# A score quad's fifth product moves to another PSUM bank, and the builder's list puts the quads' products ahead by a microsecond

## The chip, the cores and the metric

The kernel runs on one core of one Trainium2 chip. The metric is device time in microseconds (us), the median of three runs. TensorE is called PE, ScalarE ACT, VectorE DVE, GpSimd POOL; SP issues most DMAs.

## The reference, cut to what matters

One conformer block over x of shape (2, 4000, 512), all in bfloat16: a feed-forward layer, attention without heads over 4000 tokens, a convolution of three taps, and a second feed-forward layer, with layer norms between.

```python
h = _layernorm(x); h = _silu(h @ w_ff1_a) @ w_ff1_b
x1 = x + 0.5 * h
h = _layernorm(x1)
q = h @ w_q; k = h @ w_k; v = h @ w_v
scores = jnp.einsum('btd,bsd->bts', q, k) * scale
p = _softmax(scores, axis=-1)
attn = jnp.einsum('bts,bsd->btd', p, v) @ w_o
x2 = x1 + attn
...                       # convolution with gate, normalised over all tokens: x3
h = _layernorm(x3); h = _silu(h @ w_ff2_a) @ w_ff2_b
return _layernorm(x3 + 0.5 * h)
```

## The kernel before

**Tiling.** The 8000 tokens are cut into 16 chunks of 512, eight for each batch; the eighth of each batch has 416 (function `width`). Scores are computed with keys on the partitions and one chunk's queries on the free axis, 32 tiles of keys (`kt`) to a chunk (`g`).

**Stages.** The first feed-forward stage runs to about 430 us of the profile, the attention to about 1398, a short stage that finishes the convolution to about 1440, and the second feed-forward stage to the end. Convolution and layer norms of earlier chunks are laid beside the attention of later ones.

**A seven-product scheme.** Most large products use a Strassen-like scheme with seven half-size products in place of eight. In chunks that do not open a batch ("not plain", 14 of 16), four key tiles at a time form a *score quad* (`score_quad`, L1993): 7 quads to a chunk, 98 in all, each done in 4 steps, one for each `kt`. Each of its seven products is a block of 4 matmuls, 128 x 256 (128 x 208 in the two short chunks), two halves of the bank by two halves of the contraction.

**Banks of a quad.** It uses three of PSUM's eight banks: c is bank 0, x is bank 1, h is bank 2. The profile calls all of them s; y is used for the products with V and other work. Step 0: product 5 opens h, ACT copies it to m5 in SBUF, product 1 opens c, ACT copies c over h. Step 1: product 6 adds to h, DVE writes h + m5 into x (`plus`), product 2 adds to c, ACT takes the exponential of c. Step 2: product 7 adds to h, DVE writes h + m5 over m5, product 3 adds to x, ACT takes the exponentials of x and of m5. Step 3: product 4 adds to h, ACT takes its exponential. In the profile m5 has the tile name xt; the products read so: 5 and 6 are s<-xt, 1 and 2 are s<-work,keys, 7 and 4 are s<-xt,keys, 3 is s<-work,xt. DVE's sum into x is s<-s,xt, that into m5 is xt<-s,xt.

**Opening a bank.** A matmul with `start=True` opens a bank: it overwrites. Where an engine has written the bank since, a matmul with `start=False` adds to that only in columns that a matmul has written since the bank was last opened. Product 3 adds so to x, bank 1. Two users of bank 1, `q_group` (L1637) and `pw1` (L2405), write only 416 columns of it when their chunk is short; `touch` (L968) then adds a matmul of 96 columns over the rest.

**Other users of banks 0 to 2.** In chunks with quads, `sbank` gives out banks 0 and 1 in steps where quads do not hold them, and `self.bank(1)` is used by the tail keys' scores and one convolution product.

**Products with V** (`pv`, L1837) are seven forms for each pair of key tiles, into banks 3 to 7. They read the exponentials, or sums of them that DVE makes (`pair_sums`, L1796), and V or its sums, of which two forms are streamed from DRAM (xt<-v12d).

**Order of the work.** The program writes its operations into a list; a builder, `Plan`, then orders them for each engine before anything runs. A block of matmuls that ends with an increment of PE's semaphore is a node. In `once` (L272), the builder goes through the list with estimated durations; `choose("PE")` (L289) takes, among nodes whose inputs are done and that lie no more than `beside` (8000 ns) behind the head of the list, the one that can start first. Among those that can start at the same moment it takes the earliest of the list, by its number k. T[k] is the sum of the estimated PE durations ahead of node k. Other engines are ordered by how late a node may be. The best of six passes is emitted. At run time every engine goes through its own queue in order and waits on semaphores.

Every instruction is issued from one helper, so all rows of the profile have line L93; they are told apart by tiles.

Of the kernel before, what the change touches and what calls it, by code (L numbers as in the profile page):

```python
# [9 lines left out]
AF = mybir.ActivationFunctionType  # L10
AX = mybir.AxisListType

B, T, D, F, KW = 2, 4000, 512, 2048, 3
# [4 lines left out]
CHUNK = TPC * TILE  # L18
# [3 lines left out]
NCK = B * TCB  # L22
# [39 lines left out]
class Ev:  # L62
    __slots__ = ("key", "val", "snap")
# [21 lines left out]
class Call:  # L85

    __slots__ = ("name", "args", "kw")
# [16 lines left out]

class Node:

    __slots__ = ("e", "emit", "dur", "land", "preds", "succs", "left", "ready", "late", "at", "seq", "ev", "size", "turn", "other")


class Plan:  # L110
# [7 lines left out]
    def __init__(self, sync, ahead, beside):  # L118
        self.S, self.ahead, self.beside = sync, ahead, beside
        self.nodes, self.pe, self.block = [], [], []  # L120
        self.w, self.r, self.d = {}, {}, {}
        self.table, self.same, self.first = None, [], None

    @staticmethod
    def size(ap):
# [47 lines left out]
    def new(self, e, dur, land, emit, reads, writes, dkeys=()):  # L173
        n = Node()
        n.e, n.dur, n.land, n.emit, n.preds, n.succs, n.seq, n.at = e, dur, land, emit, set(), [], len(self.nodes), len(self.pe)
        n.size, n.turn, n.other = 0, False, None
        self.nodes.append(n)
        n.preds |= self.link(n, reads, writes, dkeys)
        return n
# [92 lines left out]
    def once(self):  # L272

        pe, T = self.pe, self.T
        for n in reversed(self.nodes):
            if n.e != "PE":
                n.late = min([s.late - self.lag(n, s) - (self.SPARE if n.size else 0) for s in n.succs] + [pe[min(n.at, len(pe) - 1)].late + 40000])
        free = {e: 0.0 for e in self.AFTER}
        wait = {e: [] for e in self.AFTER}
        for n in self.nodes:  # L280
            n.left, n.ready = len(n.preds), 0.0
            if not n.left:
                for e in n.other or (n.e,):
                    wait[e].append(n)
        head, done, starts = 0, [False] * len(pe), [0.0] * len(pe)
        index = {n: k for k, n in enumerate(pe)}
        order, pipe = [], 0.0

        def choose(e):  # L289
            if e == "PE":  # L290
                best = None
                for n in wait["PE"]:
                    k = index[n]
                    if T[k] - T[head] > self.beside:
                        continue
                    key = (max(free[e], n.ready - (40 if k == head else 0)), k)
                    if best is None or key < best[0]:
                        best = (key, n)
                return best and (max(free[e], best[1].ready), best[1])
            limit = T[head] + self.ahead  # L300
            found = [n for n in wait[e] if T[n.at] <= limit]
            if not found:
                return None
            now = max(free[e], min(n.ready for n in found))
            can = sorted([n for n in found if n.ready <= now], key=lambda n: (n.late, n.seq))
            soon = [n for n in found if n.ready > now]
            for n in can:
                end = now + max(n.other[e][0] if n.other else n.dur, n.size / 260) + self.OVER[e]
                if all(end <= u.ready + 60 or u.late >= end or u.late >= n.late for u in soon):
                    return now, n  # L310
            u = min(soon, key=lambda n: n.ready)
            return max(free[e], u.ready), u

        ask = dict.fromkeys(free, True)
        said = {}
        while len(order) < len(self.nodes):
            for e in free:
                if ask[e]:
                    said[e], ask[e] = choose(e), False
            e, (s, n) = min([c for c in said.items() if c[1]], key=lambda c: c[1][0])  # L320
            for o in n.other or (e,):
                wait[o].remove(n)
                ask[o] = True
            if n.other:
                self.take(n, e)
            free[n.e] = s + n.dur + self.OVER[n.e]
            order.append((n, e))
            if n.size:
                begin = max(s + (400 if n.turn else n.dur + 400), pipe)
                pipe = begin + n.size / (180 if n.turn else 260)  # L330
                n.land = pipe - s + 1000
            if n.e == "PE":
                k = index[n]
                done[k], starts[k] = True, s
                if k == head:
                    while head < len(pe) and done[head]:
                        head += 1
                    ask = dict.fromkeys(free, True)
            for u in n.succs:
                lag = self.lag(n, u)  # L340
                u.ready = max(u.ready, s if lag is None else s + lag)
                u.left -= 1
                if not u.left:
                    for o in u.other or (u.e,):
                        wait[o].append(u)
                        ask[o] = True
        return free["PE"], order, starts


class Sync:  # L350
# [125 lines left out]
    def emit_dma(self, engs, dkey, fns, reads, writes):  # L476

        req = self._required(reads, writes)
        prev = self.count[dkey]
        if prev > 0:  # L480
            v = req.get(dkey)
            if v is None or v.val < prev:
                req[dkey] = Ev(dkey, prev, {})
        for e in dict.fromkeys(engs):
            self._emit_waits(e, req)
        for e, fn in zip(engs, fns):
            fn(self.eng[e]).then_inc(self.sem[dkey], 16)
            self.count[dkey] += 16
        snap = dict(self.clock[engs[0]]) if len(set(engs)) == 1 else {}
        ev = Ev(dkey, self.count[dkey], snap)  # L490
        self._bind(ev, reads, writes)
        return ev

    def planned(self, ahead, beside):
        self.plan = Plan(self, ahead, beside)
# [55 lines left out]
class Conformer:  # L551
# [412 lines left out]
    def mm(self, out, lhsT, rhs, start, stop, reads, bank, inc=None, **kw):  # L964
        self.S.op("PE", lambda e: e.matmul(out, lhsT, rhs, start=start, stop=stop, **kw),
                  reads=reads, writes=[bank], inc=stop if inc is None else inc)

    def touch(self, ps, b_ps, W):  # L968
        if W < CHUNK and b_ps is self.bank(1)[1]:
            x = self.hT[0][:, 0, 0, :]  # L970
            self.mm(ps[:, W:CHUNK], x, x[:, 0:CHUNK - W], False, True, [self.b_hT[0][0]], b_ps, skip_group_check=True)

    def warm(self, n):

# [662 lines left out]
    def q_group(self, b, qc, dc):  # L1637

        s, sl = qc % 2, self.query_slot(b, qc)
        ps, b_ps = self.sbank()  # L1640
        W = width(qc)
        lin, lo = self.queries(qc, sl)
        for cc in range(DC):
            self.mm(ps[:, 0:W], self.M[:, cc, dc * 128:(dc + 1) * 128], lin[:, cc, lo:lo + W],
                    cc == 0, cc == DC - 1, [self.b_M] + self.b_lnT[sl], b_ps)
        self.touch(ps, b_ps, W)
        self.act(self.qT[s][:, dc, 0:W], ps[:, 0:W], AF.Copy, [b_ps], [self.b_qT[s][dc]])

    def queries(self, qc, sl):
# [343 lines left out]
    def score_quad(self, g, q, step):  # L1993
# [32 lines left out]
                 reads=[b_h, b_m5], writes=[b_out])  # L2026

        if step == 0:
            product(5, h, b_h, True)
            self.act(m5, h[:, 0:W], AF.Copy, [b_h], [b_m5])  # L2030
            product(1, c, b_c, True)
            self.act(h[:, 0:W], c[:, 0:W], AF.Copy, [b_c], [b_h])
        elif step == 1:
            product(6, h, b_h)
            plus(x[:, 0:W], b_x)
            product(2, c, b_c)
            exp(c[:, 0:W], b_c, 11)
        elif step == 2:
            product(7, h, b_h)
            plus(m5, b_m5)  # L2040
            product(3, x, b_x)
            exp(x[:, 0:W], b_x, 12)
            exp(m5, b_m5, 22)
        else:
            product(4, h, b_h)
            exp(h[:, 0:W], b_h, 21)
# [2 lines left out]

    def attention(self, old, hook):  # L2050

        for g in range(NCK):
            W, plain = width(g), g % TCB == 0
            for kt in range(KT):
# [4 lines left out]
                if plain and kt < KT - 1 or kt < 2 or kt == KT - 2:  # L2059
# [3 lines left out]
                    else:  # L2063
                        self.act(self.P30[:, 0:W], ps[:, 0:W], AF.Exp, [b_ps], [self.b_P30], scale=SCALE)
                elif not plain and kt < KT - 2:
                    self.score_quad(g, *divmod(kt - 2, 4))
                if g == 0 and kt < 2:
                    self.pop(old // 2 if kt == 0 else old - old // 2)
                if kt == (24 if g else 21):
# [335 lines left out]
    def pw1(self, t, cb, bank=None):  # L2405
# [9 lines left out]
        for out, x in moves:  # L2415
            for cc in range(DC):
                self.mm(out, self.Wp1[:, cc, cb * 128:(cb + 1) * 128], x[:, cc], cc == 0 and out is moves[0][0], cc == DC - 1,
                        [self.b_Wp1] + self.b_lnT[1 if t == NCK - 1 else 0], b_ps, skip_group_check=True)
        if t < NCK - 1:
            self.touch(ps, b_ps, W)  # L2420
        return ps, b_ps

    def taps_beside(self, t, cc):
# [603 lines left out]
```

## Time and profile before

| What | Value |
|---|---|
| Runs | 1884.49 us median of 3 (1883.29 to 1886.34) |
| Profiled execution | 1882.47 us, its span 1878.7 us |
| Granted TensorE clock | 1.0 |
| Matrix products issued | 15389 |

A row of the time order gives start, length, engine, operation, "out<-in" by tile names, shape and count, and in brackets the idle time of the engine before it and what ended that. Consecutive like instructions are merged. A row of a matmul lasts from its start to the end of its drain, so rows overlap when PE is dense. Rows of groups give count, busy us, mean ns of one, and idle time before them.

### The profile page before, as it was taken

How to read it: one execution, taken by the hardware profiler on the slowest of the kernel's cores; microseconds unless marked ns; L12 is line 12 of the kernel's file. 1: busy time of each engine (PE TensorE's matmuls, PEld its weight loads, DVE VectorE, ACT ScalarE, POOL GpSimd, SP SyncE). 2: the span in 40 equal slices, each digit the busy share in tenths (PEclk: the TensorE clock that was granted, in tenths of full speed). 3: DMA queues.
4: the chain of work that ended last, by engine and by line, in shares of the span. 5: the costliest groups of instructions: out<-in, count | busy, mean ns of one | idle time of the engine just before them, and what ended most of it. 6: DMA issues, size and time to landing. Idle time of an engine off the chain costs nothing.

```text
span 1878.7 us, 39230 instructions
## 1 busy us (share of the span) xinstructions
PE 1860.1 (99%) x15389; PEld 1442.7 (77%) x15389; DVE 1463.0 (78%) x3191; ACT 1306.9 (70%) x2419; POOL 133.2 (7%) x301
## 2 busy tenths in 40 slices
PE   9999999999999999999999999999998999999998
PEld 5888888866777777777677777777774888888886
DVE  7888888868667777776777677768778888888885
ACT  5777777644667777677667677777668687777773
POOL 1000000000000000000000000000011000000000
PEclk9999999999999999999999999999999999999999
DMA  7323344197545555447944444444375222222111
GB/s 191 101 79 91 80 113 105 57 265 214 173 144 151 158 170 166 107 133 177 248 125 133 130 122 114 122 137 121 111 203 171 74 61 71 77 46 61 49 43 33
DMA packets 325014, 231.52 MB, mean 123 GB/s; under 512 B 204179, under 2 KB 295638, under 8 KB 324566
## 3 DMA queue, kind: packets, MB, share of 16 engines
q1 hardware_dynamic: 324294, 228.68, 44.4%
q8 instruction: 123, 2.02, 0.4%
q14 instruction: 69, 0.57, 0.1%
q10 hardware_dynamic: 528, 0.26, 0.0%
HBM read 128.44 MB, written 55.79 MB: 98 GB/s over the span
## 4 chain that ended last, share of the span: by engine, by line
PE 97%; DVE 1%; ACT 1%; DMA 0%; issue 0%; DVEq 0%; ACTq 0%
PE s L93 48%; PE y L93 48%; DVE work L93 1%; ACT work L93 0%; DMA xt<-v12d 0%; DVE wff L93 0%; DVE xt L93 0%; DVE s L93 0%; ACT sums L93 0%; DMA work<-work 0%; ACT wff L93 0%; ACT keys L93 0%; ACT s L93 0%; ACT xt L93 0%; ACT L93 0%
## 5 line engine op out<-in xcount | busy, mean ns | idle before, releaser
L93 ACT ACTIVATE sums<-s 128x512 bf16<-128x512 f32 (+2 forms) x494 | 288.2, 584 | 171.3 <-PE s L93 169.9
L93 ACT ACTIVATE keys<-s 128x512 bf16<-128x512 f32 (+2 forms) x284 | 165.6, 588 | 183.6 <-PE s L93 166.4
L93 DVE TENSOR_TENSOR sums<-sums 128x512 bf16<-128x512 bf16 (+3 forms) x528 | 195.4, 398 | 75.0 <-ACT sums L93 70.0
L93 PE MATMUL y<-work,keys 128*128 128x256 bf16 x1920 | 244.6, 273 | 0.0
L93 PE MATMUL s<-work,keys 128*128 128x256 bf16 (+5 forms) x1456 | 224.5, 292 | 0.0
L93 ACT ACTIVATE work<-xt,work 128x512 bf16<-128x512 bf16 x268 | 206.7, 785 | 7.8 <-DVE work L93 7.8
L93 PE MATMUL y<-wff,keys 128*128 128x256 bf16 (+3 forms) x1592 | 209.1, 276 | 0.1
L93 PEld LDWEIGHTS y<-work,keys 128*128 128x128 bf16 x1920 | 187.8, 98 | 25.1
L93 PE MATMUL y<-sums,keys 128*128 128x256 bf16 (+1 forms) x1440 | 202.6, 270 | 0.0
L93 PE MATMUL s<-sums 128*128 128x256 bf16 x1296 | 193.8, 273 | 0.0
L93 DVE TENSOR_TENSOR keys<-keys 128x1024 bf16<-128x1024 bf16 (+2 forms) x262 | 169.2, 662 | 28.8 <-ACT keys L93 13.6
L93 PE MATMUL y<-work,wff 128*128 128x256 bf16 (+2 forms) x1116 | 184.0, 292 | 0.0
L93 PEld LDWEIGHTS y<-wff,keys 128*128 128x128 bf16 (+1 forms) x1592 | 151.2, 98 | 32.4 <-issue 3.3
L93 DVE BATCH_NORM_STATS2 work<-xt 128x6 f32<-128x512 bf16 x251 | 163.9, 680 | 5.1 <-DMA xt<-in_x_dram 4.3
L93 PEld LDWEIGHTS s<-work,keys 128*128 128x128 bf16 (+1 forms) x1456 | 119.2, 97 | 50.6 <-ACT sums L93 4.0
L93 PEld LDWEIGHTS y<-sums,keys 128*128 128x128 bf16 x1440 | 138.8, 98 | 24.1 <-DVE sums L93 0.6
L93 POOL TENSOR_TENSOR work<-work 128x4 f32<-128x4 f32 (+3 forms) x107 | 89.8, 840 | 807.4 <-DVE work L93 804.9
L93 PE MATMUL s<-work,wff 128*128 128x512 bf16 (+5 forms) x668 | 141.0, 345 | 3.2 <-DVE work L93 2.7
L93 PEld LDWEIGHTS s<-sums 128*128 128x128 bf16 x1296 | 126.7, 98 | 20.0
L93 PE MATMUL s<-work 128*128 128x512 bf16 (+4 forms) x565 | 138.5, 375 | 3.0 <-DVE work L93 1.8
L93 PE MATMUL y<-sums,xt 128*128 128x256 bf16 (+1 forms) x960 | 139.4, 270 | 1.5 <-DVE sums L93 0.8
L93 PEld LDWEIGHTS y<-work,wff 128*128 128x128 bf16 x1116 | 108.2, 98 | 29.8
(143 smaller groups left out, 3202.2 us busy)
## 6 DMA issues: line engine op xcount, KB each, us to landing
xt<-kfd SPq DMA_DIRECT2D x98, 384.0 KB, 3.3
xt<-v12d SPq DMA_DIRECT2D x105, 256.0 KB, 2.9
xd<-xt SPq DMA_DIRECT2D x28, 512.0 KB, 3.1
xt<-xd SPq DMA_DIRECT2D x28, 512.0 KB, 4.3
out_dram<-xt SPq DMA_DIRECT2D x14, 512.0 KB, 3.0
xt<-in_x_dram SPq DMA_DIRECT2D x13, 512.0 KB, 4.0
dcvd<-wff SPq DMA_DIRECT2D x48, 128.0 KB, 2.1
keys<-dcvd SPq DMA_DIRECT2D x12, 512.0 KB, 4.3
```

Of the source, the lines that this page charges most:

```text
L93: return getattr(eng, self.name)(*self.args, **self.kw)
```

## The change

Three edits go together. In `score_quad`, product 5 opens bank x (bank 1) instead of h, and ACT's copy to m5 reads it there. `touch` and its two calls are left out; product 5 now opens bank 1 over the quad's whole width before product 3 adds to it. And nodes made while a quad's step is written into the list carry `front` = 1000 (ns); among nodes that can start at the same moment, `choose` now takes the smallest T[k] - front.

```diff
@@ class Plan
+        self.front = 0
@@ def new
-        n.size, n.turn, n.other = 0, False, None
+        n.size, n.turn, n.other, n.front = 0, False, None, self.front
@@ def once, choose
-                    key = (max(free[e], n.ready - (40 if k == head else 0)), k)
+                    key = (max(free[e], n.ready - (40 if k == head else 0)), T[k] - n.front)
@@ class Sync
+    def front(self, ns):
+        if self.plan:
+            self.plan.front = ns
@@ class Conformer
-    def touch(self, ps, b_ps, W):
-        if W < CHUNK and b_ps is self.bank(1)[1]:
-            x = self.hT[0][:, 0, 0, :]
-            self.mm(ps[:, W:CHUNK], x, x[:, 0:CHUNK - W], False, True, [self.b_hT[0][0]], b_ps, skip_group_check=True)
@@ def q_group
-        self.touch(ps, b_ps, W)
@@ def score_quad
         if step == 0:
-            product(5, h, b_h, True)
-            self.act(m5, h[:, 0:W], AF.Copy, [b_h], [b_m5])
+            product(5, x, b_x, True)
+            self.act(m5, x[:, 0:W], AF.Copy, [b_x], [b_m5])
             product(1, c, b_c, True)
             self.act(h[:, 0:W], c[:, 0:W], AF.Copy, [b_c], [b_h])
@@ def attention
                 elif not plain and kt < KT - 2:
+                    S.front(1000)
                     self.score_quad(g, *divmod(kt - 2, 4))
+                    S.front(0)
@@ def pw1
-        if t < NCK - 1:
-            self.touch(ps, b_ps, W)
```

More of the change, by code (lines that the diff above doesn't have):

```diff
@@ L105 @@
 class Node:
-    __slots__ = ("e", "emit", "dur", "land", "preds", "succs", "left", "ready", "late", "at", "seq", "ev", "size", "turn", "other")
+    __slots__ = ("e", "emit", "dur", "land", "preds", "succs", "left", "ready", "late", "at", "seq", "ev", "size", "turn", "other", "front")
 class Plan:
@@ L2050, in attention @@
     def attention(self, old, hook):
+        S = self.S
         for g in range(NCK):
```

## The prediction

> **What bounds the kernel now.** I read the head of the page, its chain that ended last, and busy time by stretches (us, busy time and count of PE, PEld, DVE, ACT and POOL, granted clock, DMA share, GB/s).
>
> ```profile
> span 1878.7 us, 39230 instructions
> ...
> PE 1860.1 (99%) x15389; PEld 1442.7 (77%) x15389; DVE 1463.0 (78%) x3191; ACT 1306.9 (70%) x2419; POOL 133.2 (7%) x301
> ...
> PE 97%; DVE 1%; ACT 1%; DMA 0%; issue 0%; DVEq 0%; ACTq 0%
> ```
>
> ```profile
> 200.00:300.00 100.00, 100.00 (x918) 89.63 (x916) 89.61 (x184) 75.97 (x131) 8.06 (x8) 1.00 0.41 102
> 460.00:895.00 435.00, 432.13 (x3588) 326.92 (x3586) 320.81 (x731) 301.64 (x598) 25.27 (x83) 1.00 0.56 154
> ...
> 960.00:1398.00 438.00, 435.22 (x3673) 331.99 (x3673) 320.37 (x707) 309.95 (x609) 27.97 (x101) 1.00 0.45 127
> 1398.00:1440.00 42.00, 36.72 (x203) 17.55 (x202) 34.30 (x77) 28.97 (x53) 8.37 (x23) 1.00 0.66 210
> 1500.00:1600.00 100.00, 100.00 (x868) 84.65 (x866) 86.12 (x180) 77.48 (x136) 8.07 (x8) 1.00 0.25 70
> ```
>
> TensorE (PE) sets the end: 97% of the chain, at a granted clock of 1.00. The two feed-forward stages (200 to 300, 1500 to 1600) have no gap. The fourteen query chunks with score quads are the stretches 460 to 895 and 960 to 1398. There PE looks 99% busy, but a matmul's row contains its drain, which hides small stalls. So I went to the order of time:
>
> ```profile
> 757.33 0.61 PE L93 MATMUL s<-xt 128*128 128x256 bf16 x4
> 757.78 0.60 PE L93 MATMUL s<-work,keys 128*128 128x256 bf16 x4
> 758.05 0.70 DVE L93 TENSOR_TENSOR s<-s,xt 128x512 f32<-128x512 f32 x1 [1.20 <-PE s L93]
> 758.22 0.60 PE L93 MATMUL y<-sums,xt 128*128 128x256 bf16 x4
> ...
> 758.81 0.61 PE L93 MATMUL s<-xt,keys 128*128 128x256 bf16 x4
> 759.25 0.60 PE L93 MATMUL s<-work,xt 128*128 128x256 bf16 x4
> ...
> 759.69 1.03 PE L93 MATMUL s<-work,wff 128*128 128x512 bf16 x4
> ...
> 760.55 0.60 PE L93 MATMUL s<-xt,keys 128*128 128x256 bf16 x4
> ```
>
> This is one quad's products 6 (757.33), 2 (757.78), 7 (758.81), 3 (759.25) and 4 (760.55). Undisturbed, four 256-wide matmuls take 0.44 us of PE (757.33 to 757.78), 0.109 each, though a row of four lasts 0.60: a stall shows as idle only for what exceeds some 0.165. Product 7 starts 0.59 after the group before it, 0.15 late. It writes bank h, which VectorE (DVE) must have read. Product 6 is issued by 757.77; DVE starts 0.28 later, takes 0.70, and product 7 follows 0.06 behind: **1.04 us from 6 to 7**, in which PE needs other work, the cover. Here it had two groups, 0.87.
>
> ```profile
> PE s L93 <- DVE s L93: 2.3, 6, 0.4
> PE s L93 <- DVE xt L93: 1.5, 3, 0.6
> PE y L93 <- DVE sums L93: 0.8, 2, 0.4
> PE y L93 <- DMA xt<-v12d: 0.6, 1, 0.6
> ```
>
> ```profile
> 499.76 0.50 PE L93 MATMUL s<-xt,keys 128*128 128x256 bf16 x3 [0.21 <-DVE s L93]
> ...
> 1386.65 0.53 PE L93 MATMUL s<-xt,keys 128*128 128x208 bf16 x4
> ```
>
> The first four rows are all of PE's visible waits from 455 to 1400 (total, times, longest): 5.2 us in 12, with the hidden 0.165 each 7.2. Setting every start against the dense spacing, I find some 11 us of stalls there, apart from those at the 32-row tiles of the tail keys. Product 7 has the most: 17 stalls, 4.5 us, the first 0.37 (499.76), the last 0.22 (1386.65).
>
> **Part 1: product 5 goes to bank x.** Before, it opened bank h and so waited until ScalarE (ACT) had read product 4 of the quad before. Now it opens x, free once product 3's exponential has read it. No instruction is added.
>
> ```profile
> 761.19 0.60 ACT L93 ACTIVATE sums<-s 128x512 bf16<-128x512 f32 x1 [0.19 <-PE s L93]
> 761.42 0.61 PE L93 MATMUL y<-sums,keys 128*128 128x256 bf16 x4
> ...
> 761.93 0.60 PE L93 MATMUL s<-xt 128*128 128x256 bf16 x4
> ```
>
> Product 5 at 761.93 is 0.07 late (0.51 after a group of 0.44): product 4 (from 760.55) was issued by 760.99, and the exponential's 0.60 lies between. There are 13 such delays, 1.1 us together. In the new order product 3 leads the next product 5 by 0.7 us at least and 3.9 in the median. I take **0.9 gained**; bounds 0 and 1.1.
>
> The wait goes to what used bank 1 last. In 36 quads that is a projection or a convolution product, which DVE reads and the queue of PE, in order, now stands behind:
>
> ```profile
> L93 DVE SCALAR_TENSOR_TENSOR xt<-s,work,xt 128x512 bf16<-128x512 f32 x59 | 44.0, 746 | 14.4 <-PE s L93 14.4
> ```
>
> 0.28 + 0.75 + 0.06 is 1.09 of need, against covers of 1.06 to 1.09 in the new order: **0.3 lost**, bounds 0 and 1.1 (0.03 in each).
>
> **Part 2: quads' products lead by a microsecond.** Among groups that could start at the same moment, the builder now takes the one with the earliest place in the list, where a quad's product counts 1000 ns earlier. The new order of PE leaves the first feed-forward stage as it was up to its last chunks; in the second a few groups change place, where nothing stalls. Between them nearly every chunk is reordered, with the same matmuls. So I count the cover in each order, at 0.109 us for each 256-wide matmul. The two short chunks, with 208 columns, have their own rows:
>
> ```profile
> 874.23 0.53 PE L93 MATMUL s<-xt 128*128 128x208 bf16 x4
> 874.59 0.52 PE L93 MATMUL s<-work,keys 128*128 128x208 bf16 x4
> 875.52 0.53 PE L93 MATMUL s<-xt,keys 128*128 128x208 bf16 x4 [0.41 <-DVE s L93]
> ```
>
> Product 6 takes 0.36 (0.089 a matmul), and 7 follows its issue at 874.59 by 0.93: the need there.
>
> Product 6 to 7: the old order is short of 1.03 us (0.93 in the short chunks) in 17 of 98 quads, by 4.45 us, which agrees with the 4.5 seen. The new one is short in three quads, by 0.3, and in four by 0.05 since m5 comes late. **4.0 gained**, bounds 3.0 and 4.2.
>
> Product 1 to 6 goes through ACT's copy of c to h:
>
> ```profile
> 763.23 0.60 PE L93 MATMUL s<-work,keys 128*128 128x256 bf16 x4
> 763.67 0.60 PE L93 MATMUL s<-sums,keys 128*128 128x256 bf16 x4
> 764.10 0.60 PE L93 MATMUL y<-sums,keys 128*128 128x256 bf16 x4
> 764.56 0.61 PE L93 MATMUL s<-xt 128*128 128x256 bf16 x4
> ```
>
> Two groups of cover (763.67, 764.10) leave product 6 late by 0.02, so 0.89 is needed. In the new order 27 quads have just these 0.87 and one 0.44, 1.1 us short together against 0.2 in the old: **0.9 lost**, bounds 0.6 and 1.2. Product 7 to 4 needs what 6 to 7 needs; three quads of the short chunks now lack 0.62 together, against 0.06: **0.6 lost**, bounds 0 and 0.6.
>
> The Trainium skill speaks against counting cover so: "TensorE: Matmul & The Clock Gate", section Back-to-back issue gap, gives some 131 ns per 512-wide matmul in a stream of weight loads and matmuls. By it, product 3 and one such group would cover an estimated 0.96 us between 7 and 4, some 0.07 short in every quad that has just these. The trace differs: from 759.69 to 760.55 four of them take 0.86, 0.215 each.
>
> **Part 3: products with V, and the rest.**
>
> ```profile
> 502.57 0.38 PE L93 MATMUL y<-sums,xt 128*128 128x256 bf16 x2 [0.45 <-DVE sums L93]
> ...
> 1376.81 0.35 PE L93 MATMUL y<-sums,xt 128*128 128x208 bf16 x2 [0.64 <-DMA xt<-v12d]
> ```
>
> Products with V that come early wait for DVE's sums over a quad's exponentials: three stalls, 1.3 us, the first 0.61 (502.57). From product 4 to the first of them the new order has 6.8 us of PE work in the mean instead of 5.5, and 0.7 at least instead of 0.2. **1.2 gained**, bounds 0 and 1.3. The wait for V's transfer (1376.81, 0.81) stays: in that place the release of its buffer leads its use by 4.6 us in both orders.
>
> ```profile
> 781.80 0.42 ACT L93 ACTIVATE work<-work 128x256 bf16<-128x256 bf16 x1 [2.72 <-DMA work<-work]
> ...
> 784.18 0.61 PE L93 MATMUL s<-xt,keys 128*128 128x256 bf16 x4 [0.51 <-DVE xt L93]
> ```
>
> In four chunks product 4 of the first quad is late (2.2 us together), as at 784.18: ACT stood behind a transposing transfer, and DVE behind ACT. Nothing in the change speeds that transfer up: 0, bounds 2.2 either way.
>
> ```profile
> L93 PE MATMUL s<-keys 128*128 128x96 bf16 x5 | 1.0, 204 | 0.0
> ```
>
> The removed matmuls are these five: 96 columns at 0.109 per 256 are 0.04 each, **0.2 gained**, bounds 0 and 1.0.
>
> **The sum.** Gains 0.9 + 4.0 + 1.2 + 0.2 = 6.3, losses 0.3 + 0.9 + 0.6 = 1.8: 4.5 us. The profiled execution took 1882.5 us, its span and 3.8 around it, so 1878.0; the median shown lies 2.0 above it, at 1884.5, so I forecast **1880.0**.
>
> **Rivals.** *More of it goes.* Quads that run earlier may also lift the four late product 4s and the last 0.9 of product 5 and V: of some 11 us about 9.5 would go, giving 1875. For it: the covers grow nearly everywhere. Against it: the transfer is no part of the change.
>
> *The stalls only move.* Covers are PE work; they suffice only if DVE and ACT take each operation at once, and these are 73 and 70% busy in the stretches. If one in ten of the 98 quads finds a 0.4 to 0.7 us operation ahead of its sum, 10 x 0.5 gives 5 back: 1884.5. Against it: in the old order covers alone explain product 7's stalls to 0.1 us.
>
> *Slower: bank 1's reader.* In the 36 quads of part 1 the margin is nil. If DVE has one operation of 0.69 ahead of that read, product 5 and all PE work behind it are that much later. From 7 such quads the gain is gone (7 x 0.69 = 4.8); at 13 the kernel is slower by over 0.2%; at half of them, 18 x 0.69 - 4.5 gives 1892. For it: DVE, unlike ACT in the old place, reads most projections behind other sums. Against it: before, product 1 stood behind the same reader on bank 0, and stalls there come to 0.2 us.
>
> **How the numbers follow.** The forecast gets 0.52, more of it 0.14, no net change 0.24, the slower case 0.10. About 0.2%, 3.8 us, is what a measurement of this kernel can tell from no change. Gains over it: 0.44 of the forecast's 0.52 and the whole second case, 0.58; within it the other 0.08, the third case's 0.22 and a little of the last: 0.30; slower 0.12. The forecast's own bounds are 1875.5 to 1883.5. The range 1874.5 to 1887.5 takes in the second case and the third, and leaves out the slow end.
>
> **What would show it.** Right: the visible waits of PE for DVE s fall from 2.3 us to below 0.5; product 5's matmuls (s from xt) follow their predecessor at 0.44; rows for s from keys with 96 columns are gone; many product 6 rows 0.02 late. Wrong: idle time before s from xt released by DVE xt or DVE work at chunks' steps with projections, sums on DVE that start over 0.3 after product 6, or new stalls in the stage after the last chunk (now 1398 to 1440), which should keep its gaps of 5.3 us. The forecast falls if the stretches 460 to 895 and 960 to 1398 together do not shrink by 2 us or more.

## The result, and the profile after

The changed kernel took 1878.73 us (median of 9 runs, 1877.09 to 1879.83) against 1883.55 us before (9 runs, 1882.21 to 1886.34): a ratio of 0.9975, 95% interval 0.9967 to 0.9984. The profiled execution took 1879.46 us, its span 1875.7.

The head of its page, and busy time by stretches (columns as before):

```profile
span 1875.7 us, 39058 instructions
...
PE 1851.9 (99%) x15271; PEld 1444.6 (77%) x15384; DVE 1465.4 (78%) x3188; ACT 1309.2 (70%) x2421; POOL 134.6 (7%) x302
```

```profile
460.00:895.00 435.00, 431.16 (x3573) 329.24 (x3604) 324.05 (x734) 303.25 (x601) 23.36 (x83) 1.00 0.56 154
960.00:1393.00 433.00, 430.13 (x3617) 330.60 (x3645) 318.27 (x701) 308.99 (x607) 29.48 (x101) 1.00 0.45 129
1393.00:1436.00 43.00, 37.62 (x200) 18.36 (x202) 34.77 (x76) 28.86 (x52) 9.45 (x24) 0.96 0.65 205
```

This trace lacks 113 matmul rows (15271, where 15384 weights were loaded), so PE's busy time reads some us too low and proves nothing here. What can be read is when things happen. The last matmul of the chunks with score quads started at 1397.94 us before and starts at 1393.22 now, so 4.7 us went there. The stage behind it keeps its gaps (43.00 - 37.62 = 5.4 us, 5.3 before), but from that matmul to the end of the span 1.7 us more pass than before: in this execution the granted clock is 0.5 for 3.4 us from 1428.2 us on (hence the 0.96 in the row above), which costs some 0.8 us, and the new order waits 0.66 us for ACT before the matmul at 1445.46. Hence 3.0 us in the spans.

The same quad's place in the order of time:

```profile
751.88 0.60 PE L93 MATMUL s<-xt,keys 128*128 128x256 bf16 x4
752.32 0.60 PE L93 MATMUL s<-xt 128*128 128x256 bf16 x4
...
754.31 0.61 PE L93 MATMUL s<-xt 128*128 128x256 bf16 x4
754.76 0.60 PE L93 MATMUL s<-work,keys 128*128 128x256 bf16 x4
...
755.19 0.60 PE L93 MATMUL s<-sums,keys 128*128 128x256 bf16 x4
...
755.63 0.38 PE L93 MATMUL y<-sums,xt 128*128 128x256 bf16 x2
...
755.85 0.60 PE L93 MATMUL s<-xt,keys 128*128 128x256 bf16 x4
```

Product 5 (752.32) follows product 4 of the quad before at 0.44, without a wait for its exponential. Between product 6 (754.31) and product 7 (755.85) stand two and a half groups instead of two, 1.09 us from the issue of 6 (754.76 to 755.85), and 7 is on time. PE's visible waits from 455 to 1400 us:

```profile
PE s L93 <- DVE xt L93: 2.3, 3, 1.8
PE s L93 <- ACT sums L93: 0.4, 2, 0.3
PE s L93 <- ACT s L93: 0.4, 1, 0.4
```

The waits for DVE s (2.3 us) are gone, and so are those of the products with V. Most of what is left is one stall of product 4, in the first quad of the chunk at 835 us:

```profile
835.66 2.75 SPq L93 DMA_TRANSPOSE work<-work  x2
...
841.85 0.42 ACT L93 ACTIVATE work<-work 128x256 bf16<-128x256 bf16 x1 [3.46 <-DMA work<-work]
...
844.30 0.53 PE L93 MATMUL s<-xt,keys 128*128 128x208 bf16 x4 [1.84 <-DVE xt L93]
```

### The profile page after: what moved, and what is told of

The parts are those of the page before. It is cut to its first block, busy times and chain, and to the rows that moved or that the text cites. A ratio compares the mean times of both kernels' runs of the same rounds, so it can differ in the third digit from the quotient of the medians.

```text
span 1875.7 us, 39058 instructions
## 1 busy us (share of the span) xinstructions
PE 1851.9 (99%) x15271; PEld 1444.6 (77%) x15384; DVE 1465.4 (78%) x3188; ACT 1309.2 (70%) x2421; POOL 134.6 (7%) x302
## 3 DMA queue, kind: packets, MB, share of 16 engines
q8 instruction: 123, 2.02, 0.4%
## 4 chain that ended last, share of the span: by engine, by line
PE 95%; ACT 2%; DVE 1%; DMA 1%; issue 1%; POOL 0%; SPq 0%; DVEq 0%; ACTq 0%
PE y L93 48%; PE s L93 47%; DVE work L93 1%; ACT work L93 1%; ACT sums L93 1%; DMA work<-work 0%; DVE xt L93 0%; DMA xt<-in_x_dram 0%; POOL work L93 0%; ACT keys L93 0%; ACT xt L93 0%; DVE s L93 0%; DVE wff L93 0%; ACT wff L93 0%; ACT s L93 0%
## 5 line engine op out<-in xcount | busy, mean ns | idle before, releaser
L93 PE MATMUL s<-work,keys 128*128 128x256 bf16 (+5 forms) x1430 | 219.7, 290 | 1.9 <-ACT sums L93 0.4
L93 PE MATMUL y<-sums,keys 128*128 128x256 bf16 (+1 forms) x1440 | 212.6, 270 | 0.0
L93 PE MATMUL y<-wff,keys 128*128 128x256 bf16 (+2 forms) x1590 | 208.7, 276 | 0.4 <-DVE xt L93 0.4
L93 PE MATMUL y<-work,wff 128*128 128x256 bf16 (+2 forms) x1116 | 188.6, 292 | 0.0
L93 PE MATMUL y<-sums,xt 128*128 128x256 bf16 (+1 forms) x960 | 145.6, 270 | 0.0
L93 PE MATMUL s<-work 128*128 128x512 bf16 (+4 forms) x513 | 122.9, 374 | 5.8 <-DVE work L93 1.4
L93 PE MATMUL s<-xt,keys 128*128 128x256 bf16 (+1 forms) x816 | 124.3, 270 | 2.6 <-DVE xt L93 2.3
```

Source lines behind the costliest of these rows:

```text
L93: return getattr(eng, self.name)(*self.args, **self.kw)
```

## The experiments

For every kernel the stalls were taken as in the prediction: each start of a PE matmul set against the dense spacing, in the chunks with score quads. "All" includes some 14 us at 32-row tiles (17.6 in one kernel, named below); matmuls whose rows are missing were counted by the order in which they stand.

| Kernel | us, median | product 7 | product 4 | product 5 | 6 and 1 | V | all |
|---|---|---|---|---|---|---|---|
| before | 1883.55 | 4.5 | 2.3 | 1.1 | 0.8 | 2.1 | 27.7 |
| changed | 1878.73 | 0.9 | 3.0 | 1.0 | 2.1 | 0.0 | 23.3 |
| bank_only | 1881.66 | 0.5 | 6.0 | 1.2 | 0.5 | 1.0 | 26.5 |
| front_only | 1882.39 | 5.5 | 1.3 | 0.4 | 1.8 | 1.0 | 27.0 |
| front_300 | 1882.47 | 1.7 | 5.5 | 0.8 | 1.0 | 0.3 | 26.0 |
| front_4000 | 1886.03 | 1.2 | 0.7 | 2.2 | 3.9 | 0.3 | 30.0 |
| after_k240 | 1877.79 | 0.9 | 2.5 | 1.0 | 2.1 | 0.0 | 22.8 |
| after_k32 | 1882.09 | 0.9 | 4.6 | 1.0 | 2.1 | 0.2 | 25.1 |
| bank_only_k233 | 1879.83 | 0.5 | 2.6 | 1.7 | 0.5 | 0.5 | 23.5 |
| before_k228 | 1884.45 | 4.5 | 2.1 | 1.3 | 0.8 | 1.9 | 27.7 |
| after_late1700 | 1876.57 | 0.3 | 0.7 | 1.6 | 1.2 | 0.2 | 21.3 |
| after_late1700_k32 | 1876.08 | 0.3 | 0.7 | 1.6 | 1.2 | 0.2 | 20.4 |
| bank_only_late1700 | 1879.63 | 0.3 | 0.4 | 4.9 | 2.3 | 0.2 | 24.5 |
| before_late1700 | 1883.88 | 1.5 | 1.2 | 2.4 | 3.6 | 1.1 | 26.6 |

The kernel before took 1883.4, 1884.3, 1883.7 and 1882.9 us in the four sets of experiments, in the order below. Every ratio is to the kernel before in the same set; medians of different sets can be compared to about a microsecond only.

### One part alone, and other leads

bank_only has the change without the lead:

```diff
-                    S.front(1000)
                     self.score_quad(g, *divmod(kt - 2, 4))
-                    S.front(0)
```

front_only has the lead, with product 5 on h and `touch` as before; front_300 and front_4000 are the changed kernel with `S.front(300)` and `S.front(4000)`.

> Only the first edit: product 5 opens bank x, no touching matmuls, no lead in the list. Theory 'the bank': what made products late was that four of a quad's products and an exponential went through bank h in turn; with product 5 on x the builder finds covers without any lead. In this kernel's order the covers named in the prediction (6 to 7, 1 to 6, 7 to 4, the exponential to 5, readers of banks 0 and 1) lack 2.6 us in sum, against 8.0 in the order of before and 3.9 in the changed kernel: 4 to 6 us faster than before, as fast as the changed kernel within 1.5 us. Rival 'the lead' (as the prediction's part 2 put it, 4.0 of the gain comes with the microsecond): at most 1.5 us faster than before.

> Only the second edit: product 5 stays on bank h and the touching matmuls stay, quads' products get the lead of 1000 ns. 'The bank': the covers in this order still lack 6.8 us (product 6 to 7 alone 4.8 in 18 quads), so 0 to 1.5 us faster than before. 'The lead': 3 to 4 us faster.

> The changed kernel with a lead of 300 ns in place of 1000. 'The bank': by the covers in its order (2.3 us lacking, the least) 5 to 6 us faster than before, up to 1.5 us faster than the changed kernel. 'The lead': a third of the lead gives a part of its gain, 2 to 3 us faster than before.

> The changed kernel with a lead of 4000 ns. 'The bank': more products 6 follow product 1 too closely (34 of 98 quads, 1.9 us), the covers lack 4.5 us in sum: 3 to 4 us faster than before, 0.5 to 1.5 slower than the changed kernel. 'The lead': as fast as the changed kernel or faster.

Measured, as ratios to before: bank_only 0.9991 (0.9982 to 1.0000), front_only 0.9998 (0.9989 to 1.0007), front_300 1.0000 (0.9991 to 1.0009), front_4000 1.0011 (1.0002 to 1.0020). Neither part alone gives what both give, and both theories missed. By the medians bank_only gained 1.8 us instead of the first theory's 4 to 6 (the second's bound was 1.5), front_only 1.0 instead of the second's 3 to 4 (the first's bounds were 0 and 1.5), front_300 1.0, below both, and front_4000 lost 2.6 where both had a gain. But the stalls behind the totals are clear. One quad of bank_only, then the corresponding one of front_only:

```profile
755.88 0.60 PE L93 MATMUL s<-xt 128*128 128x256 bf16 x4
756.32 0.60 PE L93 MATMUL s<-work,keys 128*128 128x256 bf16 x4
756.76 0.60 PE L93 MATMUL y<-sums,keys 128*128 128x256 bf16 x4
757.19 0.38 PE L93 MATMUL y<-sums,xt 128*128 128x256 bf16 x2
757.41 0.60 PE L93 MATMUL s<-xt,keys 128*128 128x256 bf16 x4
```

```profile
757.90 0.61 PE L93 MATMUL s<-xt 128*128 128x256 bf16 x4
758.35 0.60 PE L93 MATMUL s<-work,keys 128*128 128x256 bf16 x4
758.78 0.38 PE L93 MATMUL y<-sums,xt 128*128 128x256 bf16 x2
759.38 0.61 PE L93 MATMUL s<-xt,keys 128*128 128x256 bf16 x4 [0.21 <-DVE s L93]
```

The bank alone puts 1.09 us between the issue of product 6 and product 7 (756.32 to 757.41), and 7 is dense; the lead alone leaves one and a half groups there (758.35 and 758.78), and 7 is late. The table says so for all quads: 0.5 us against 5.5. Over all orders, product 7 has 0.3 to 1.7 us with the bank, and 4.5, 5.5 and, in before_late1700, 1.5 without it: the bank makes covers easier to find, and an order can come near without it. Yet bank_only gives it back at product 4, as its visible waits show:

```profile
PE s L93 <- DVE xt L93: 4.7, 5, 1.6
```

front_4000 reorders so much that its tile switches cost 17.6 us instead of 14, and product 6 has 3.2 us of stalls. Of the three leads that were tried with the bank, 1000 is the fastest, but front_300 has 2.5 us more of product 4's stalls, and the next part gives those another cause.

### Why product 4 is late: the instruction blocks

Product 4 of a chunk's first quad stands behind ACT's reduction of the softmax sums, which stands behind two transposing transfers. In the first six kernels the reduction starts 3.8 us after these are issued, the first and the eighth chunk left aside, where it is always later. Where ACT waited longer for the transfers, it started up to 1.9 us later (2.4 once). Of these 27 late reductions, 23 had a 16 KB packet of queue q8, marked "instruction", starting 0.9 to 3.4 us after the issue (the other four are of front_4000, which issues the two transfers further apart than the usual 1.24 us); of the 39 that started within 4.1 us of the issue, none had. Such packets come about every 14.7 us in the median, 123 in a span (packets, MB, share of the 16 DMA engines):

```profile
q8 instruction: 123, 2.02, 0.4%
```

The Trainium skill ("Runtime: NRT & Kernel Launch", section Instruction fetch mechanics) says that an engine's code is streamed in blocks of 16 KiB, 256 instructions, by its sequencer's own DMA queue, at a cost that is mostly hidden. The trace agrees in size (2.02 MB over 123) and number (two instructions for each of 15384 matmuls, over 256, give 120). What it costs is what the next four kernels test. They keep every matmul in its order and add satisfied waits in the first feed-forward stage alone, one instruction each (39058 instructions become 39298 with 240), so that the block boundaries fall elsewhere:

```diff
         req = self._required(reads, writes)
+        if e == "PE":
+            self.n_pe += 1
+            if self.n_pe >= 600 and self.n_pe % 6 == 0 and self.extra < 240 and not any(
+                    self.clock[e].get(k, 0) < ev.val for k, ev in req.items() if k != e):
+                self.extra += 1
+                for k in ("ACT", "DVE", "POOL"):
+                    self.eng[e].wait_ge(self.sem[k], 1)
         self._emit_waits(e, req)
```

The number is 240 or 32 on the changed kernel, 233 on bank_only and 228 on the kernel before.

> The order of all matmuls is that of the changed kernel; 240 satisfied waits in the first feed-forward stage only move the points at which TensorE's instruction blocks (16 KB, one per about 14.7 us) are fetched, here to about 0.9 us later against the attention stretches. Theory 'blocks' (a block fetched 0.9 to 3.4 us after the two transposes of a chunk's sums are issued delays ScalarE's reduction from +3.8 us to as much as +5.7 us, and product 4 with it): no chunk's reduction starts later than 4.2 us after the issue, the 2.0 us stall of product 4 near 842 us is gone, product 4 stalls come to less than 1 us against 3.0, and the attention stretches end about 2 us sooner. Total 1876 to 1878 us if the waits themselves cost nothing, up to 3 us more if they do not hide. Rival 'order' (late product 4s come from the order of the matmuls or the traffic of the data queues): the stall stays, total within 0.5 us of the changed kernel's 1878.7 apart from the cost of the waits.

> As the previous kernel with 32 waits, which put the blocks about 1.8 us earlier than in the changed kernel. Theory 'blocks': four other chunks (the 5th, 6th, 12th and 13th) get a block 1 to 3.4 us behind their transposes; their reductions start 4.5 to 5.7 us after the issue, product 4 stalls come to 4 to 6 us against 3.0, and the total is 1 to 3 us above the changed kernel's: 1879.7 to 1881.7 us. Rival 'order': within 0.5 us of 1878.7 us.

> Product 5 on the third product's bank and nothing else of the change, with 233 satisfied waits in the first feed-forward stage that put the blocks about 1.3 us later. Theory 'blocks': the late product 4s of bank_only (6.0 us, of which 1.5, 1.8 and 1.3 us in three chunks) fall to below 3 us, and the total falls from 1881.7 us to about 1878 to 1879, apart from the cost of the waits: the bank alone is then worth nearly the whole change. Rival 'order' (without the lead the order itself leaves product 4 late): the 6.0 us stay, 1881.2 to 1882.2 us.

> The kernel before in its own order, with 228 satisfied waits in the first feed-forward stage that put the blocks about 1.6 us later, where no chunk's transposes meet one. Theory 'blocks': product 4 stalls fall from 2.3 to below 0.5 us while the 4.5 us of product 7 stay, and the total falls by 2 us from 1883.5 to 1881 to 1882, apart from the cost of the waits. Rival 'order': 1883 to 1884 us.

Measured: after_k240 0.9961 (0.9948 to 0.9975), after_k32 0.9984 (0.9975 to 0.9993), bank_only_k233 0.9975 (0.9965 to 0.9984), before_k228 1.0001 (0.9992 to 1.0010). Between the first two, whose matmuls are the same in the same order, lie 4.3 us. In their profiled executions 2.3 of it is in the chunks with score quads, and 0.9 is one stall for DVE at 336 us in the feed-forward stage. That stall is of the same kind: DVE waits 1.82 us there for a pair of transposes issued at 327.73, with a block 3.3 us behind (331.05). The remaining 1.1 us is not the blocks': in after_k32's profiled execution the granted clock is 0.5 for 3.4 us from 1430.2 us on, and in after_k240's it stays at 1.0 there. The runs agree: with a granted clock of 1.0 over the span, four runs of after_k240 took 1876.6 to 1877.9 us and two of after_k32 1879.6 and 1879.9, some 2 us apart. In after_k32 the four chunks named were late, their reductions at 5.3 to 5.6 us, and the last one too (5.7); the total was 0.4 us above its bounds. In the four kernels with waits, 11 of 12 late reductions have a block 0.9 to 3.4 us behind the issue, and none of the 35 that came within 4.1 us. One of them, the thirteenth, in the changed kernel and in after_k32, by the order of time:

```profile
1210.70 2.50 SPq L93 DMA_TRANSPOSE work<-work  x2
...
1214.48 0.42 ACT L93 ACTIVATE work<-work 128x256 bf16<-128x256 bf16 x1 [0.18 <-DMA work<-work]
...
1218.28 0.60 PE L93 MATMUL s<-xt,keys 128*128 128x256 bf16 x4
```

```profile
1212.59 2.50 SPq L93 DMA_TRANSPOSE work<-work  x2
...
1218.01 0.42 ACT L93 ACTIVATE work<-work 128x256 bf16<-128x256 bf16 x1 [1.82 <-DMA work<-work]
...
1220.56 0.61 PE L93 MATMUL s<-xt,keys 128*128 128x256 bf16 x4 [0.23 <-DVE xt L93]
```

3.78 us from issue to reduction become 5.42, and product 4, on time before, waits. And the transfers between these points, in 40 equal slices (1210.70 to 1214.50 us, then 1212.59 to 1218.00 us), with the queues:

```profile
GB/s 22 11 0 0 0 0 0 0 0 0 0 0 59 199 221 232 213 216 175 60 6 0 0 0 0 0 92 216 216 229 216 213 159 39 3 0 0 0 0 0
...
q1 hardware_dynamic: 1093, 0.27, 34.4%
issues: line engine op xcount, KB each, median us to landing
work<-work SPq DMA_TRANSPOSE x2, 2.4
```

```profile
GB/s 341 167 53 0 0 0 0 0 28 185 221 216 216 97 6 0 0 121 64 206 206 208 178 44 0 0 0 0 2 8 9 9 9 9 15 98 242 265 311 53
...
q1 hardware_dynamic: 1322, 0.47, 57.4%
q8 instruction: 1, 0.02, 1.8%
issues: line engine op xcount, KB each, median us to landing
dcvd<-wff SPq DMA_DIRECT2D x1, 128.0 KB, 2.0
work<-work SPq DMA_TRANSPOSE x2, 3.3
```

Both show the two transposes as two bursts at some 215 GB/s; what stands at the two ends of the second window belongs to other transfers (dcvd is issued at 1216.46). In the second there is one block, from 1214.94 to 1216.51, and once it is over a rest of the transposes follows at 9 GB/s, to about 1217.3, in packets of 256 bytes that start one after another, some 0.03 us apart. That is near the rate of one of the 16 DMA engines (215 / 16 is 13) with the other 15 done, as would be if the block had held that engine; the records do not name a packet's engine, so this last step is argued. By the Trainium skill ("DMA: Bandwidth & Descriptors", section Queues, rings and completion order) a DMA engine takes turns between its queues by whole packets; the trace fits that, with a block that takes 0.9 us at the least and 1.57 here.

after_k240 fell by 0.9 us instead of 2, within its bounds for the total (1876 to 1878) but not for product 4 (2.5 us instead of less than 1): the chunk at 835 us was hit again (its reduction at 6.0 us, product 4 late by 1.8), since the block moved only from 2.7 to 3.5 us behind the issue, and in both an 8 KB block of queue q14 comes before it. bank_only_k233 did as expected in kind (product 4 from 6.0 to 2.6 us), the total 0.8 us above its bounds. before_k228 missed: two chunks were freed, but the chunk at 840 us was hit (product 4 late by 1.56), and the feed-forward stage, where the waits stand, has a new stall of 1.3 us for DVE (at 312.9 us, again behind a pair of transposes, with a block 3.9 us behind their issue).

With equal delays the lead's share can be read too. Chunk by chunk, the reduction's start after the issue and the stall of product 4 behind it:

| Chunk | bank_only | with the lead |
|---|---|---|
| sixth | 5.34, 1.50 | 5.32, 0.62 (after_k32) |
| thirteenth | 5.53, 1.76 | 5.42, 0.39 (after_k32) |
| fourteenth | 5.08, 1.31 | 5.39, 0.36 (changed) |

The lead gives product 4 some 0.9 to 1.3 us more room; where no block falls behind the transposes, it gives next to nothing in these orders. All stalls but product 4's come to 20.4 and 21.0 us in the two kernels with the bank alone, and to 20.3 to 20.5 in the three with the lead.

### Room for the transposes

If late transposes are the cause, an order that reckons them longer should not feel the blocks. The builder's line in `once`, on the changed kernel, on it with the 32 waits, on bank_only and on the kernel before:

```diff
-                n.land = pipe - s + 1000
+                n.land = pipe - s + (1000 + 1700 if n.turn else 1000)
```

> The changed kernel whose builder reckons every transposing transfer 1.7 us longer, so that product 4 of a chunk's first quad is put that much further behind its transposes. Theory 'blocks' (a block fetched behind the transposes makes them up to 1.9 us late; the order has less room than that): product 4 stalls fall from 3.0 to below 1 us wherever the blocks fall, the other stalls of the attention stretches stay near 20 us, total 1876 to 1878 us. Rival 'order' (product 4 is late because the list puts it early by the matmuls' own times, or the room is taken from other products): product 4 stays above 2 us or other stalls grow by as much, total 1878 to 1880 us.

> The previous kernel with the 32 satisfied waits that cost the changed kernel 3.4 us (1882.1 us against 1878.7). Theory 'blocks': reductions in several chunks still start 5 us or later after the issue, but with 1.7 us of room they cost product 4 less than 1 us in all, and the total is within 1 us of the previous kernel's. If the 3.4 us came from the waits' own time or from other transfers, the total is again 2.5 to 4 us above the previous kernel's.

> Product 5 on the third product's bank, no lead, and the builder's 1.7 us more for transposing transfers. Theory 'the bank carries the gain, the lead only loosens product 4': product 7 stalls stay below 0.6 us, product 4 stalls fall from 6.0 to below 1 us, and the total falls from 1881.7 us to 1876.5 to 1879 us, beside the changed kernel without any lead. Rival 'the lead is needed': total stays above 1880 us.

> The kernel before (product 5 on the first product's bank, no lead) with only the builder's 1.7 us more for transposing transfers. Theory 'three parts' (the margin takes away the stalls of product 4, the bank those of product 7, and neither does the other's work): product 4 stalls fall from 2.3 to below 1 us, product 5 and 7 together keep 4 us or more, total 1880.5 to 1882.5 us. Rival 'the margin alone' (any order with room behind the transposes is as good as the changed kernel's): product 5 and 7 together below 2.5 us, total 1877 to 1879.5 us.

Measured: after_late1700 0.9958 (0.9944 to 0.9971), after_late1700_k32 0.9958 (0.9944 to 0.9971), bank_only_late1700 0.9976 (0.9966 to 0.9986), before_late1700 1.0003 (0.9994 to 1.0012). The two hits are the first ones: 1876.6 and 1876.1 us, and the 32 waits, with which the changed kernel was slower (3.4 us by the medians, 1.7 by the ratios), cost nothing. The same chunk and the visible waits of after_late1700:

```profile
1209.46 2.51 SPq L93 DMA_TRANSPOSE work<-work  x2
...
1216.04 0.41 ACT L93 ACTIVATE work<-work 128x256 bf16<-128x256 bf16 x1
```

```profile
PE s L93 <- DMA work<-work: 0.9, 1, 0.9
PE s L93 <- ACT s L93: 0.3, 1, 0.3
PE s L93 <- DVE xt L93: 0.2, 1, 0.2
```

The reduction comes 6.6 us after the issue by ACT's own order, without idle time ahead of it, and PE waits for DVE xt 0.2 us instead of 2.3 (the 0.9 us is one other wait, which after_late1700_k32 does not have). By the medians this version beats the changed kernel by 2.2 us; their intervals against the kernel before just overlap.

bank_only_late1700 lost its product 4 stalls (0.4) but got 4.9 us at product 5, and missed its range by 0.6 us: with room for the transposes the lead is worth 3 us, since the order without it runs short elsewhere. before_late1700 answers whether room alone is enough. It is not, as the visible waits of that kernel show:

```profile
PE s L93 <- ACT s L93: 2.5, 3, 0.9
PE s L93 <- ACT sums L93: 1.3, 3, 0.7
```

Products 7 and 4 fall to 1.5 and 1.2 us, and products 5 and 6, which on h and behind m5 wait for ACT, rise to 2.4 and 3.3 (products 5 and 7 together 3.9, product 4 a little above its bound). Its total missed for another reason: its span was 1.2 us shorter than that of the kernel before (medians 1877.8 and 1879.0), but 6.2 us lie around the span, where all other kernels have 3.9 to 4.2. That stays open.

## Why the prediction came true, and where its steps were wrong

The forecast was 1880.0 us and 1878.73 was measured; 0.9 of the 1.3 us between them lies in the start, which three runs had put at 1884.49 and nine put at 1883.55. The sum was 4.5 us, 0.2 of it for the five matmuls that are gone; 4.4 us of stalls went (27.7 to 23.3), and the median fell by 4.8. The sum is right, but the cause of its largest term is not, and it comes out so close partly by luck: its terms are off by some 1.7 us one way and 1.6 the other, as listed here, 0.6 of that in groups that the sum does not name.

- **Product 5 on bank x, 0.9 gained:** thirteen waits for ScalarE became one of 0.07 us. Right.
- **Bank 1's reader, 0.3 lost:** 33 waits of 0.01 to 0.10 us, 1.0 together. The mechanism is right and the size was taken too low, within its bounds. No quad found a VectorE operation of 0.69 in front; the slower rival did not happen.
- **Product 6 to 7, 4.0 gained by the lead:** this step failed in its cause. 3.6 us went (4.5 to 0.9), within the bounds, but the runs show no part of the lead in it: the lead alone leaves 5.5 us, the bank alone 0.5. The step read the cover from the finished order and gave it to the part of the change that speaks of order. The builder moves groups as soon as a bank is free earlier; why that leaves more groups there was not traced in the builder.
- **Product 1 to 6, 0.9 lost:** product 6 lost 0.55 us net, with one new stall of 0.60 before the matmul at 1002.25 us, and product 1 another 0.8, most of it in the last chunk (0.71 in two stalls). Right in sign, and the second place was not foreseen.
- **Product 7 to 4, 0.6 lost:** 0.38 us in a short chunk, as expected, and 0.28 in one other quad. Right in sum.
- **V, 1.2 gained:** 2.1 went. The wait for V's transfer, which was to stay (0.81 us), is gone.
- **Late product 4s, 0 within 2.2:** 2.2 us before, 2.4 after. The value was right by luck. "Nothing in the change speeds that transfer up" was true, but any change that adds or removes PE instructions moves the blocks that slow it down: in the same order of matmuls, product 4 costs 2.5 us in after_k240 and 4.6 in after_k32, and with the stall at 336 us some 3 of the 4.3 us between the totals go back to the blocks, two thirds of the forecast gain. The rival in which more of it goes is what happens when these four get room: 1876.6 us.
- **Touch, 0.2 gained:** no row of s from keys with 96 columns is left.

Counting covers alone, as the prediction did, put bank_only 4 to 6 us ahead; it does not see a transfer whose length depends on what else is fetched at the time.

## What to carry to other kernels

Where an order is made by a list builder, run each part of a change alone before giving a gain to one of them: here a choice of buffer did the reordering. A chain through a DMA needs room for its late case, and the late case is found by setting the same step side by side over all its repetitions. And before believing a difference of a few us between two orders, move the instruction blocks with a few satisfied waits in a quiet stage; if the time moves, a part of the difference was their place. Compare the granted clock too: 3.4 us at half clock cost as much as several of the stalls named here.

## What was not expected of the hardware

A fetch of PE's code, 16 KB at a time, makes a pair of transposing DMAs late by up to 1.9 us (their reader starts 5.7 us after the issue instead of 3.8; 6.2 once, with a second, 8 KB block ahead of it) and through them PE by up to 2.0, in whichever chunks it falls 0.9 to 3.4 us behind their issue. That it does so by holding one of the 16 DMA engines is argued, not shown. Two hundred and forty satisfied waits in a dense PE stage cost no time that can be seen there: the stage's stalls are 4.8 us with them and 4.9 without.
